# A searched start order, idle products inside the first banks, and an earlier release of v

## The chip, the cores and the metric

The kernel runs on one core of a Trainium2 chip. The metric is device time in microseconds (us), the median of several executions. One execution was also recorded by the hardware profiler; its times are counted from the start of its span.

## What is computed

Two steps follow each other. The first is a gated linear recurrence over 4 sequences of 768 tokens with 8 heads of width 48; the second is a feed-forward layer of 384 to 2048 to 384 with a GELU.

```
state = zeros(B, H, D, D)                      # B, H, S, D = 4, 8, 768, 48
for t in range(S):
    state = alpha[:, :, t, :, None] * state + einsum('bhd,bhe->bhde', k[:, :, t], v[:, :, t])
    y[:, :, t] = einsum('bhd,bhde->bhe', q[:, :, t], state)
x = y.transpose(0, 2, 1, 3).reshape(B * S, H * D)      # 3072 x 384
out = gelu_tanh(x @ w_in) @ w_out                      # w_in 384 x 2048, w_out 2048 x 384
```

## The kernel before

**Tiling.** A sequence is cut into 6 chunks of 128 tokens. A chunk of one sequence is a unit; two sequences at the same chunk are a pair, so there are 12 pairs, numbered 0 to 11, with units 0 and 1 in each. Pairs 0 and 1 are the first chunk of all four sequences.

**Steps of a pair.** Every step has a name: its kind, the pair (or block of the feed-forward layer), a dot and a running number.
- `ln` takes the logarithm of alpha (ScalarE, L359). `cum` sums it over the tokens by products (TensorE, L346 and L350 for pairs 0 and 1). `b`, `binv` and `bend` are exponentials of that sum (ScalarE, L407 and L401). `qp` and `kp` multiply q and k by them (VectorE, L418).
- `t` turns qp or kp by TensorE (L428), and `ev` copies the result out of its bank (L446, ScalarE or VectorE). In pairs 0 and 1, t 0 and 1 turn q and k of unit 0, t 2 and 3 those of unit 1, and t 4 and 5 turn k back for both units (L454, copies on L461).
- `attn` makes k times q (L489), and `mask` multiplies by a triangle (VectorE, L496; two for each unit). `vb` converts v to bf16 (L389). `y` multiplies the masked tile by vb (L546), `x` copies y out (L553), `tx` turns it (L560), `xe` copies it into the input of the feed-forward layer (L564).
- `kv` makes the state's addition (L506), `end` the factors at the chunk's end (L516), `st` the new state (L531).

**Feed-forward steps.** `l1` followed by a block number and a running number makes two of the sixteen hidden strips for one pair: six products of 256 columns (L572); `gelu` follows on ScalarE (L578). l10.0 to l10.7 is block 0 (pair 0), l11.0 to l11.7 block 1. Strips l10.0 and 1 need the first quarter of w_in, l10.2 and 3 the second, l10.4 and 5 the third, l10.6 and 7 the fourth. `l2` adds four strips into the result of one unit (L591), `ot` copies it out, `store` writes it.

**Banks.** PSUM tiles come from three rings: `ca` (1), `yk` (2 banks, shared by t, kv, y and tx) and `ff` (4 banks, shared by l1, l2, the first cums, some attn and idle products). A step that takes a bank waits until the copy that empties it is done.

**Order.** The program is recorded by a scheduler class. The order of the first 46 us or so is written out in `FIRST` (L186): each word is an engine (P TensorE, V VectorE, A ScalarE, G GpSimd, S SyncE) and a step. `fill.n` is n idle products of 512 columns of zeros into an ff bank (L289). Engines work strictly in that order, each on its own. What comes behind `FIRST` the scheduler orders by priorities and its own costs; `LANDED` (L203) tells it when loads are taken to land, for this ordering alone.

**Loads.** The twelve 192 KB loads of alpha, q and k for pairs 0 and 1 (load.0 to load.11) go out from SyncE, but for load.2 and load.3 (q and k of unit 0), which go out from ScalarE. All others go out from GpSimd in the order of `LOADS`: load.12 is v of pair 0, then come the first quarter of w_in, v of pair 1, the other quarters, w_out and the later pairs. A `gate` is a one-column copy on GpSimd (L314) out of a tile that has to have landed: what GpSimd issues behind it waits with it. `gatea 0 1` is a copy out of alpha of unit 1 of pair 0 and stands ahead of v of pair 0; `gatek 0 1` is one out of k of unit 1 and stands ahead of w_in.

Of the kernel before, what the change touches and what calls it, by code (L numbers as in the profile page):

```python
# [171 lines left out]
class _Kernel:  # L172
# [3 lines left out]

    SPLIT = (2,)
    EARLY = (0, 1)
    LOADS = ('gatea 0 1', 'v0', 'gatek 0 1', 'in 0', 'v1', 'in 1', 'in 2', 'in 3', 'out 0', 'out 1', '2a', 'out 2', '2b', 'out 3', '3', '4', '5', '6', '7', '8', '9', '10', '11')

    PACKED, CUM_FF, R = (0, 1), (0, 1), 4
    RINGS = (('a', 0, 0, 1), ('a', 0, 1, 2), ('q', 0, 0, 1), ('k', 0, 0, 1), ('q', 0, 1, 2), ('k', 0, 1, 2),
             ('a', 1, 0, 1), ('a', 1, 1, 2), ('q', 1, 0, 1), ('k', 1, 0, 1), ('q', 1, 1, 2), ('k', 1, 1, 2))
    BY_ACT = (2, 3,)

    FIRST = """  # L186
        A:table.0 A:load.2 A:load.3 S:load.0 S:load.1 S:load.4 A:ln0.0 S:load.5 P:fill.7 P:cum0.0 A:ln0.1 G:gate.0 G:load.12 S:load.6 P:cum0.1 A:b0.0 S:load.7
        A:bend0.0 V:qp0.0 A:binv0.0 A:binv0.1 S:load.8 V:kp0.0 P:fill.2 P:t0.0 A:b0.1 V:ev0.0 P:fill.1 P:t0.1 S:load.9 A:ev0.1 V:qp0.1 S:load.10 A:bend0.1
        P:fill.3 P:attn0.0 V:kp0.1 G:gate.1 S:load.11 P:t0.2 G:load.13 V:mask0.0 A:ev0.2 P:t0.3 G:load.14 V:mask0.1 A:ev0.3 P:fill.1 P:t0.4 V:ev0.4 P:fill.1
        P:attn0.1 A:ln1.0 G:load.15 P:t0.5 V:mask0.3 P:cum1.0 A:ev0.5 G:load.16 V:vb0.0 A:ln1.1 V:end0.0 P:y0.0 V:mask0.2 G:load.17 P:kv0.0 A:binv1.0 P:cum1.1  # L190
        V:st0.0 A:x0.0 G:load.18 A:vb0.1 V:kp1.0 P:tx0.0 A:b1.0 P:y0.1 V:xe0.0 G:load.19 V:qp1.0 P:t1.1 A:x0.1 A:bend1.0 G:load.20 A:b1.1 P:fill.1 P:t1.0
        A:ev1.0 V:ev1.1 G:load.21 V:qp1.1 P:fill.1 P:kv0.1 V:st0.1 G:load.22 A:binv1.1 P:tx0.1 P:attn1.0 V:xe0.1 G:load.23 P:t1.2 V:kp1.1 P:l10.0 A:ev1.2
        G:load.24 V:mask1.0 P:t1.3 A:bend1.1 P:t1.4 V:mask1.1 G:load.25 A:ev1.3 P:l10.1 V:ev1.4 G:load.26 A:vb1.0 P:t1.5 P:attn1.1 G:load.27 V:ev1.5 P:y1.0
        G:load.28 P:l10.3 V:end1.0 V:vb1.1 V:mask1.2 G:load.29 A:gelu0.0 P:kv1.0 P:l10.2 V:mask1.3 A:x1.0 G:load.30 P:l10.5 A:gelu0.1 V:st1.0 A:gelu0.3 P:y1.1
        G:load.31 P:l10.4 A:gelu0.5 V:x1.1 P:tx1.0 A:gelu0.2 P:tx1.1 P:l10.6 G:load.32 V:xe1.1 A:gelu0.4 V:xe1.0 P:l10.7 A:gelu0.6 G:load.33 P:l11.0 A:gelu0.7
        P:l11.6 A:gelu1.0 P:l11.5 A:gelu1.6 P:l11.7 A:gelu1.5 P:l11.2 A:gelu1.7 P:l11.4 A:gelu1.2 P:l11.3 A:gelu1.4 P:l11.1 A:gelu1.3 P:kv1.1 P:l20.0
        A:gelu1.1 P:l20.4 P:l20.1 A:ln2.0 P:l20.2 P:cum2.0 P:l20.5 A:b2.0 A:binv2.0 P:l20.9 A:bend2.0 V:kp2.0 A:ln2.1 P:l20.6 V:st1.1 P:cum2.1 V:qp2.0 P:l20.8
        A:b2.1 A:binv2.1 P:t2.0 P:l20.3 V:kp2.1 A:ev2.0 V:qp2.1 P:l20.10 A:bend2.1 P:attn2.0 P:t2.1 V:mask2.1 P:l20.7 A:ev2.1 V:mask2.0 P:l20.14 A:ln3.0
        P:attn2.1 P:y2.0 V:mask2.2 P:l20.13 V:mask2.3 P:l20.12 V:x2.0 P:cum3.0 A:ot0.0 V:ot0.1 P:y2.1 A:ot0.2 S:store0.0 S:store0.1 P:tx2.0 P:l20.11 A:x2.1
        S:store0.2 V:xe2.0 A:b3.0 P:tx2.1 P:l20.15 V:xe2.1 A:binv3.0 V:end2.0 P:l12.0 V:ot0.3 A:bend3.0 P:l12.1 V:qp3.0 S:store0.3 P:kv2.0 P:l12.2 V:st2.0  # L200
        A:gelu2.0 P:l12.3 V:end3.0 V:kp3.0 A:gelu2.1 P:l12.4 A:gelu2.2 P:t3.0 A:gelu2.3 P:t3.1 A:gelu2.4 V:ev3.0 P:l12.5
    """.split()
    LANDED = {"load.0": 2800, "load.1": 3400, "load.2": 4400, "load.3": 5000, "load.4": 6000, "load.5": 7300, "load.12": 10100, "load.6": 9200, "load.7":  # L203
              10000, "load.8": 10500, "load.9": 11000, "load.10": 11600, "load.11": 12000, "load.13": 14100, "load.14": 16000, "load.15":
              17800, "load.16": 19200, "load.17": 21100, "load.18": 23500, "load.19": 24800, "load.20": 26400, "load.21": 27100, "load.22":
              27900, "load.23": 28300, "load.24": 30100, "load.25": 31000, "load.26": 31900, "load.27": 32600, "load.28": 32900, "load.29":
              34800, "load.30": 36700, "load.31": 38400, "load.32": 41200, "load.33": 42600}

    NARROW = (0, 1)

# [12 lines left out]
                a=6, q=5, k=5, vb=6)  # L223
# [60 lines left out]
    def fill(self, n):  # L284
# [4 lines left out]
                self.nc.tensor.matmul(ps, self.zero[:, 0:self.C], self.zero, start=True, stop=True)  # L289
        return emit  # L290


    def load(self, n, c, i, lo=0, hi=2):

# [202 lines left out]
                                         self.ut[:, None, :].to_broadcast([self.C, self.H // 2, self.C]), op=ALU.mult)  # L497
        return emit

    def kv(self, u, i):  # L500
        nc, H, C, D = self.nc, self.H, self.C, self.D

        def emit(e):
            kv = u["kv", i] = self.tile("yk", [C, H // 2, 2 * D], F32, "kv")
            for p in range(H // 2):
                nc.tensor.matmul(kv[:, p, :], u["kn" if u["packed"] else "kp"][:, i, 2 * p:2 * p + 2, :].rearrange("t h d -> t (h d)"),  # L506
                                 u["vb"][:, i, 2 * p:2 * p + 2, :].rearrange("t h d -> t (h d)"),
                                 start=True, stop=True)
        return emit
# [25 lines left out]
    def y(self, u, i, c, b):  # L535
        nc, H, C, D = self.nc, self.H, self.C, self.D

        def emit(e):
            y = u["y", i] = self.tile("yk", [C, H, D], F32, "yps")
            if c > 0:  # L540
                st = self.state[b][c % 2]
                for p in range(H // 2):
                    nc.tensor.matmul(y[:, 2 * p:2 * p + 2, :], u["T"][:, 0, i, p, :], st[:, p, :],  # L543
                                     start=p == 0, stop=False, skip_group_check=True)
            for h in range(H):
                nc.tensor.matmul(y[:, h, :], u["atm", i][:, h % 2, h // 2, :], u["vb"][:, i, h, :],  # L546
                                 start=c == 0, stop=True, skip_group_check=True)
        return emit
# [4 lines left out]
            self.copy(e)(x, u["y", i].rearrange("t h d -> t (h d)"))  # L553
        return emit

    def turn_x(self, u, i):
        def emit(e):
            ps = u["xT_ps", i] = self.tile("yk", [self.C, self.NKT, self.C], BF16, "xT_ps")
            for j in range(self.NKT):
                self.nc.tensor.transpose(ps[:, j, :], u["x", i][:, j * self.C:(j + 1) * self.C], self.ident)  # L560
        return emit
# [57 lines left out]
    def tasks(self):  # L619
        s = self.s = Scheduler(self.BUFS, self.fill, 60000, self.FIRST, self.LANDED)  # L620
# [6 lines left out]
        loads, n, gate, held = {}, 0, [], {}  # L627
# [43 lines left out]
        for m, (c, i) in enumerate(pairs):  # L671
# [81 lines left out]
            for j in range(2):  # L753
                b, o, k, ms, turned = 2 * i + j, P + 10 + 3 * j, kp[j], masks[j], turns[j]
                at = ats[m][-1 if m not in self.SINGLE else j]
                y = s.add("y", {"PE": W["intra"] + (W["inter"] if c else 0)}, P + 20 + j, self.y(u, j, c, b),
                          ms + turned + [vin[j]] + ([states[b, c - 1]] if c else []))
                xc = s.add("x", {"ACT": W["xc_act"], "DVE": W["xc"]}, P + 20 + j, self.x(u, j), [y])
                if m in self.TURN_X:
                    xe = tx = s.add("turn", {"SP": W["turn"]}, P + 22 + j, self.turn_x_dma(u, j, c, b), [xc], xbar=W["xbar_x"], late=W["late_x"] * (m < 6))  # L760
                else:
                    tx = s.add("tx", {"PE": W["tx"]}, P + 22 + j, self.turn_x(u, j), [xc])
                    xe = s.add("xe", {"DVE": W["xe"]}, P + 22 + j, self.turned_x(u, j, c, b), [tx])
                    tx.take("yk", xe)
                y.take("yk", xc)
                xc.take("x", tx)
                users += [at, y]
                ms[0].take("atm", y)
                xts[c, b], ys[b, c] = xe, y
                vs.append(y)  # L770
                if c < NCH - 1:
                    if u["packed"]:
                        tb = s.add("t", {"PE": W["t4"]}, P + 29 + j, self.turn_back(u, j), turned)
                        k = s.add("ev", {"DVE": W["ev4"], "ACT": W["ev4_act"]}, P + 29 + j, self.turned_back(u, j), [tb])
                        tb.take("yk", k)
                        users.append(tb)
                        backs.append(tb)
                    kv = s.add("kv", {"PE": W["kv"]}, P + 30 + j, self.kv(u, j), [k, vin[j]])
                    st = states[b, c] = s.add("st", {"DVE": W["st" if c else "st0"]}, P + 30 + j, self.carry(u, j, c, b),
                                              [kv, end] + ([states[b, c - 1], ys[b, c - 1]] if c else []))  # L780
                    kv.take("yk", st)
                    vs.append(kv)
                    kvs.append(kv)
                    cs.append(st)
# [136 lines left out]
```

## Time and profile before

| | |
|---|---|
| median of 6 runs | 177.3 us (176.57 to 178.02) |
| profiled execution | 178.02 us |
| its span | 176.3 us |
| TensorE busy | 170.8 us (97%) |
| ScalarE, VectorE, GpSimd busy | 128.9, 96.4, 57.7 us |
| longest groups | l1 products (L572) 69.7 us, l2 products (L591) 69.0 us |
| DMA | 28.86 MB, mean 164 GB/s |

The span is the stretch that the profiler records; 1.7 us of the execution's time lie outside it. In the lists below, "x6" is the number of instructions put together in a row, and what stands in brackets is the idle time ahead of the row on its engine, with what ended it. In the DMA views q0 is GpSimd's queue, q1 SyncE's and q10 ScalarE's.

### The profile page before, as it was taken

The page shows a single profiled execution, that of the slowest core. Times are in us where ns is not written, and L with a number is a line of the kernel's source. Part 1 is how long each engine was busy: PE and PEld are TensorE (multiplying, and loading weights), DVE is VectorE, ACT ScalarE, POOL GpSimd, SP SyncE. Part 2 cuts the span into 40 slices and gives each one's busy share as a digit, 9 for nine tenths or more (in the row PEclk, how much of TensorE's full clock was granted, in tenths as well). Part 3 has the DMA queues.
Part 4 walks back from the last instruction along what each step waited for, and adds up shares of the span by engine and source line. Part 5 has one row for each costly group of instructions (what it writes and reads, how often), then busy time and mean ns, then how long its engine had stood idle before and what let it go on. Part 6 is the DMA issues. An engine that isn't in the chain of part 4 may idle for free.

```text
span 176.3 us, 4440 instructions
## 1 busy us (share of the span) xinstructions
PE 170.8 (97%) x1845; PEld 135.0 (77%) x1845; DVE 96.4 (55%) x192; ACT 128.9 (73%) x213; POOL 57.7 (33%) x64
## 2 busy tenths in 40 slices
PE   7899899999999999999999999999999999999993
PEld 2566799666986897797698688688697697796973
DVE  6499820166878995696499797494436405000000
ACT  4678979756968667858788967987988984481841
POOL 2495347996646766576620000000000000000000
PEclk9999999999999999999999999999999999999999
DMA  4999999999999999999999991271271360301102
GB/s 142 309 247 202 210 244 235 234 218 203 235 292 206 237 259 222 208 226 205 195 259 232 204 159 52 58 172 53 47 176 38 89 164 4 105 29 45 48 0 89
DMA packets 49620, 28.86 MB, mean 164 GB/s; under 512 B 37696, under 2 KB 46016, under 8 KB 49600
## 3 DMA queue, kind: packets, MB, share of 16 engines
q0 software_dynamic: 26464, 17.70, 60.8%
q1 hardware_dynamic: 22592, 10.49, 23.3%
q10 hardware_dynamic: 544, 0.39, 0.8%
q8 instruction: 14, 0.23, 0.5%
q14 instruction: 6, 0.05, 0.1%
HBM read 25.17 MB, written 4.72 MB: 170 GB/s over the span
## 4 chain that ended last, share of the span: by engine, by line
PE 86%; DMA 9%; POOL 2%; SPq 1%; issue 0%; ACT 0%; POOLq 0%
PE acc L591 36%; PE hT L572 35%; DMA w_in<-in_moe_w_in_dram 6%; PE at L489 3%; DMA k<-in_k_dram 3%; PE qkT_ps L428 3%; PE yps L546 2%; PE yps L543 2%; PE cum L378 2%; PE kv L506 2%; SPq L305 1%; PE xT_ps L560 1%; POOL w_in L321 1%; PE cum L380 1%; POOL v L308 1%
## 5 line engine op out<-in xcount | busy, mean ns | idle before, releaser
L572 PE MATMUL hT<-xT,w_in 128*128 128x256 bf16 x576 | 69.7, 273 | 0.5 <-DMA w_in<-in_moe_w_in_dram 0.5
L578 ACT ACTIVATE gT<-hT 128x512 bf16<-128x512 f32 x96 | 56.5, 598 | 18.5 <-PE hT L572 15.1
L591 PE MATMUL acc<-w_out,gT 128*128 128x384 bf16 (+3 forms) x416 | 69.0, 313 | 0.0
L572 PEld LDWEIGHTS <-w_in 128*128 128x128 bf16 x576 | 61.0, 114 | 2.5 <-DMA w_in<-in_moe_w_in_dram 0.9
L591 PEld LDWEIGHTS <-gT 128*128 128x128 bf16 x416 | 36.9, 97 | 19.2
L496 DVE TENSOR_TENSOR atm<-at,ut 128x512 bf16<-128x512 f32 x48 | 30.1, 681 | 12.7 <-PE at L489 12.6
L418 DVE TENSOR_TENSOR qp<-q,b 128x768 bf16<-128x768 f32 (+1 forms) x15 | 11.9, 794 | 13.9 <-ACT b L407 13.8
L418 DVE TENSOR_TENSOR kp<-k,binv 128x768 bf16<-128x768 f32 (+1 forms) x15 | 11.9, 792 | 11.1 <-ACT binv L407 10.6
L603 ACT COPY ot<-acc 128x384 f32<-128x384 f32 (+3 forms) x17 | 7.4, 439 | 13.0 <-PE acc L591 12.9
L308 POOL DMA_DIRECT2D k<-in_k_dram x11 | 12.2, 1108 | 7.5 <-DVE atm L496 2.3
L308 POOL DMA_DIRECT2D q<-in_q_dram x11 | 12.2, 1108 | 6.7 <-DVE qp L418 1.3
L308 POOL DMA_DIRECT2D a<-in_alpha_dram x11 | 12.2, 1114 | 5.5 <-DMA w_in<-in_moe_w_in_dram 1.3
L308 POOL DMA_DIRECT2D vb<-in_v_dram x11 | 12.1, 1104 | 5.1 <-DMA a<-in_alpha_dram 2.3
L407 ACT ACTIVATE b<-cum 128x768 bf16<-128x768 f32 (+1 forms) x15 | 10.3, 685 | 3.2 <-PE cum L380 2.3
L280 ACT ACT_TABLE_LOAD x9 | 11.5, 1283 | 0.9 <-PEq L905 0.7
L578 ACT ACT_TABLE_LOAD x9 | 11.5, 1283 | 0.2
L407 ACT ACTIVATE binv<-cum 128x768 bf16<-128x768 f32 (+1 forms) x15 | 10.2, 682 | 0.0
L528 DVE TENSOR_TENSOR stmp<-kv,st 128x384 f32<-128x384 f32 x16 | 8.8, 552 | 2.0 <-PE kv L506 2.0
L553 DVE CAST x<-yps 128x384 bf16<-128x384 f32 x12 | 6.7, 556 | 5.8 <-PE yps L546 5.7
L446 ACT COPY qkT<-qkT_ps 128x512 bf16<-128x512 bf16 (+1 forms) x9 | 6.5, 728 | 4.1 <-PE qkT_ps L428 4.1
L531 DVE TENSOR_TENSOR st<-stmp,ends 128x384 bf16<-128x384 f32 x16 | 8.9, 558 | 0.6
L546 PE MATMUL yps<-vb,atm 128*128 128x48 bf16 x192 | 8.7, 183 | 0.1
(65 smaller groups left out, 155.7 us busy)
## 6 DMA issues: line engine op xcount, KB each, us to landing
out_dram<-ot SPq DMA_DIRECT2D x19, 192.0 KB, 4.8
a<-in_alpha_dram POOLq DMA_DIRECT2D x9, 384.0 KB, 11.7
q<-in_q_dram POOLq DMA_DIRECT2D x9, 384.0 KB, 11.6
k<-in_k_dram POOLq DMA_DIRECT2D x9, 384.0 KB, 11.6
vb<-in_v_dram POOLq DMA_DIRECT2D x9, 192.0 KB, 11.7
w_in<-in_moe_w_in_dram POOLq DMA_DIRECT2D x4, 384.0 KB, 10.0
w_out<-in_moe_w_out_dram POOLq DMA_DIRECT2D x4, 384.0 KB, 11.4
out_dram<-ot SPq DMA_DIRECT2D x9, 96.0 KB, 1.8
```

The costliest lines, as they stand in the source:

```text
L280: nc.scalar.add_instruction(mybir.InstLoadActFuncSet(name=nc.get_next_instruction_name(), act_func_set_id=i, engine=mybir.EngineType.Activ ...
L308: dma(u[t][:, lo:hi].rearrange("t b h d -> t (b h) d"), src.rearrange("b h s d -> s (b h) d")[c * C:(c + 1) * C])
L407: self.nc.scalar.activation(u[n].rearrange("t i h d -> t i (h d)")[:, lo:hi], cum, AF.Exp, scale=1.0 if n == "b" else -1.0)
L418: self.nc.vector.tensor_tensor(out, rows, b, op=ALU.mult)
L496: self.nc.vector.tensor_tensor(u["atm", i][:, o], u["at", i][o], self.ut[:, None, :].to_broadcast([self.C, self.H // 2, self.C]), op=ALU.mult)
L528: nc.vector.tensor_tensor(s, acc, old, op=ALU.add)
L531: nc.vector.tensor_tensor(new.rearrange("f p (o d) -> f (p o) d", o=2), acc.rearrange("f p (o d) -> f (p o) d", o=2), ends, op=ALU.mult)
L546: nc.tensor.matmul(y[:, h, :], u["atm", i][:, h % 2, h // 2, :], u["vb"][:, i, h, :], start=c == 0, stop=True, skip_group_check=True)
L572: self.nc.tensor.matmul(h[:, s], w_in[:, j, nt % 4 + s], self.xT[c % self.NX][:, j, lo:hi].rearrange("p g t -> p (g t)"), start=j == 0, st ...
L578: return lambda e: self.nc.scalar.activation(self.gT[c % self.NG][:, nt:nt + 2, lo * self.C:hi * self.C], f.pop(("h", c, lo, nt)), AF.Gelu ...
L591: self.nc.tensor.matmul(f["acc", c, b][:, lo:hi], self.gT[c % self.NG][:, nt, b * self.C:(b + 1) * self.C], self.w_out[:, nt, lo:hi], star ...
L603: self.copy(e)(f["ot", c, b][:, sl], f["acc", c, b] if half is None else f["acc", c, b, half][:, sl])
```

## The change

There are four edits.
- The first gate copies out of alpha of unit 0 instead of alpha of unit 1, so v of pair 0 may be issued when the first alpha has landed.
- `FIRST` and `LANDED` are replaced. The order of the loads on SyncE, ScalarE and GpSimd stays the same up to load.48. On the other engines the start is reordered. On ScalarE ln1.0 and ln1.1 now stand ahead of ev0.2 (before: behind ev0.3 and behind ev0.5). On VectorE qp1.0 and kp1.0 stand ahead of vb0.0, mask0.2 and mask0.3. On TensorE cum1.0 and cum1.1 stand ahead of attn0.1, t1.0 ahead of y0.0, kv0.1 behind attn1.1 (before: ahead of tx0.1), and l10.0 to 7 and kv1.1 as the diff shows. Eight copies change between ScalarE and VectorE. Some steps of blocks 1 to 4 change places.
- Five single idle products (`fill.1`) are left out; fill.7, fill.2 and fill.3 stay.
- `WARM` puts idle products into the bank of the first y, kv and tx, ahead of the real ones: two ahead of each y of pair 0 and one ahead of kv0.0, of 384 columns of zeros, and four transposes of the identity ahead of each tx of pair 0. They use the bank that the step takes anyway and are overwritten by it.

The diff, cut to the rows of `FIRST` that reach into block 1:

```
-    LOADS = ('gatea 0 1', 'v0', 'gatek 0 1', 'in 0', 'v1', 'in 1', 'in 2', ...
+    LOADS = ('gatea 0 0', 'v0', 'gatek 0 1', 'in 0', 'v1', 'in 1', 'in 2', ...
...
+    WARM = {("y", 0): 2, ("kv", 0): 1, ("y", 1): 2, ("tx", 0): 4, ("tx", 1): 4}
     FIRST = """
-        A:table.0 A:load.2 A:load.3 S:load.0 S:load.1 S:load.4 A:ln0.0 S:load.5 P:fill.7 P:cum0.0 A:ln0.1 G:gate.0 G:load.12 S:load.6 P:cum0.1 A:b0.0 S:load.7
-        A:bend0.0 V:qp0.0 A:binv0.0 A:binv0.1 S:load.8 V:kp0.0 P:fill.2 P:t0.0 A:b0.1 V:ev0.0 P:fill.1 P:t0.1 S:load.9 A:ev0.1 V:qp0.1 S:load.10 A:bend0.1
-        P:fill.3 P:attn0.0 V:kp0.1 G:gate.1 S:load.11 P:t0.2 G:load.13 V:mask0.0 A:ev0.2 P:t0.3 G:load.14 V:mask0.1 A:ev0.3 P:fill.1 P:t0.4 V:ev0.4 P:fill.1
-        P:attn0.1 A:ln1.0 G:load.15 P:t0.5 V:mask0.3 P:cum1.0 A:ev0.5 G:load.16 V:vb0.0 A:ln1.1 V:end0.0 P:y0.0 V:mask0.2 G:load.17 P:kv0.0 A:binv1.0 P:cum1.1
-        V:st0.0 A:x0.0 G:load.18 A:vb0.1 V:kp1.0 P:tx0.0 A:b1.0 P:y0.1 V:xe0.0 G:load.19 V:qp1.0 P:t1.1 A:x0.1 A:bend1.0 G:load.20 A:b1.1 P:fill.1 P:t1.0
-        A:ev1.0 V:ev1.1 G:load.21 V:qp1.1 P:fill.1 P:kv0.1 V:st0.1 G:load.22 A:binv1.1 P:tx0.1 P:attn1.0 V:xe0.1 G:load.23 P:t1.2 V:kp1.1 P:l10.0 A:ev1.2
-        G:load.24 V:mask1.0 P:t1.3 A:bend1.1 P:t1.4 V:mask1.1 G:load.25 A:ev1.3 P:l10.1 V:ev1.4 G:load.26 A:vb1.0 P:t1.5 P:attn1.1 G:load.27 V:ev1.5 P:y1.0
-        G:load.28 P:l10.3 V:end1.0 V:vb1.1 V:mask1.2 G:load.29 A:gelu0.0 P:kv1.0 P:l10.2 V:mask1.3 A:x1.0 G:load.30 P:l10.5 A:gelu0.1 V:st1.0 A:gelu0.3 P:y1.1
-        G:load.31 P:l10.4 A:gelu0.5 V:x1.1 P:tx1.0 A:gelu0.2 P:tx1.1 P:l10.6 G:load.32 V:xe1.1 A:gelu0.4 V:xe1.0 P:l10.7 A:gelu0.6 G:load.33 P:l11.0 A:gelu0.7
...
+        A:table.0 S:load.0 S:load.1 A:load.2 S:load.4 A:load.3 S:load.5 S:load.6 A:ln0.0 P:fill.7 P:cum0.0 S:load.7 A:ln0.1 G:gate.0 G:load.12 S:load.8
+        P:cum0.1 A:b0.0 A:binv0.0 S:load.9 V:qp0.0 A:bend0.0 A:bend0.1 V:kp0.0 A:b0.1 P:fill.2 P:t0.0 S:load.10 A:binv0.1 V:ev0.0 P:t0.1 G:gate.1 S:load.11
+        G:load.13 A:ev0.1 V:end0.0 V:qp0.1 G:load.14 A:ln1.0 P:fill.3 P:attn0.0 V:kp0.1 P:t0.2 A:ln1.1 V:mask0.1 P:cum1.0 A:ev0.2 G:load.15 V:mask0.0 P:t0.3
+        A:b1.0 P:t0.4 P:cum1.1 V:ev0.3 G:load.16 A:binv1.0 A:ev0.4 V:qp1.0 P:t0.5 G:load.17 P:attn0.1 V:kp1.0 A:ev0.5 P:t1.0 G:load.18 V:vb0.0 A:ev1.0
+        V:mask0.2 P:y0.0 G:load.19 A:x0.0 P:t1.1 V:mask0.3 A:ev1.1 P:kv0.0 G:load.20 V:vb0.1 V:st0.0 A:binv1.1 P:y0.1 G:load.21 A:x0.1 V:kp1.1 P:tx0.0
+        G:load.22 A:bend1.0 P:tx0.1 V:xe0.0 A:b1.1 P:attn1.0 G:load.23 V:xe0.1 P:t1.3 V:qp1.1 P:l10.0 G:load.24 A:ev1.3 V:mask1.1 P:t1.2 A:bend1.1 G:load.25
+        P:t1.4 V:mask1.0 A:ev1.2 P:l10.1 G:load.26 V:ev1.4 A:vb1.0 P:t1.5 G:load.27 P:attn1.1 V:ev1.5 P:kv0.1 G:load.28 V:st0.1 G:load.29 P:l10.2 V:end1.0
+        V:mask1.3 A:gelu0.0 G:load.30 P:kv1.0 A:vb1.1 P:l10.3 V:st1.0 A:gelu0.1 P:y1.0 V:mask1.2 P:l10.4 G:load.31 A:x1.0 A:gelu0.2 P:kv1.1 P:l10.5 V:st1.1
+        A:gelu0.3 G:load.32 P:y1.1 A:gelu0.4 P:tx1.0 P:l10.6 V:x1.1 A:gelu0.5 G:load.33 V:xe1.0 P:tx1.1 P:l10.7 A:gelu0.6 V:xe1.1 P:l11.0 A:gelu0.7 P:l11.1
...
+    def warm(self, key, bank, c, b):
+        width = bank.shape[1] * bank.shape[2]
+        for _ in range(self.WARM.get((key, b), 0) if c == 0 else 0):
+            self.nc.tensor.matmul(bank, self.zero[:, 0:self.C],
+                                  self.zero[:, 0:width].rearrange("p (a b) -> p a b", a=bank.shape[1]), start=True, stop=True)
...
             kv = u["kv", i] = self.tile("yk", [C, H // 2, 2 * D], F32, "kv")
+            self.warm("kv", kv, c, b)
...
             y = u["y", i] = self.tile("yk", [C, H, D], F32, "yps")
+            self.warm("y", y, c, b)
...
             ps = u["xT_ps", i] = self.tile("yk", [self.C, self.NKT, self.C], BF16, "xT_ps")
+            for _ in range(self.WARM.get(("tx", b), 0) if c == 0 else 0):
+                self.nc.tensor.transpose(ps[:, 0, :], self.ident, self.ident)
```

## The prediction

> **What bounds the kernel now.** I read the chain of work that ended last first, because TensorE is 97% busy and the share alone does not say what it is worth.
>
> ```profile
> 2.87 5.14 DMA k<-in_k_dram
> 8.05 0.09 issue
> 8.14 0.18 POOL gate L314
> 8.32 0.29 issue
> 8.61 0.74 POOL w_in L321
> 9.35 1.17 POOL v L308
> 10.52 0.73 POOL w_in L321
> 11.25 10.56 DMA w_in<-in_moe_w_in_dram
> 21.85 0.85 PE hT L572 x6
> ```
>
> The end is set by TensorE only from 21.85 us on. Until then it is set by loads: k of unit 1 lands at 8.01, the second gate opens, GpSimd issues the quarters of w_in, and the third quarter lands 10.56 us after its issue, at 21.8. By the DMA answers for each issue the four quarters land at 15.5, 19.95, 21.8 and 23.7. The stretches show that after this nothing is free on TensorE:
>
> ```profile
> 24.00:28.00 4.00, 4.00 (x39) 4.00 (x38) 0.56 (x2) 3.38 (x7) 1.98 (x3) 1.00 1.27 239
> 60.00:100.00 40.00, 40.00 (x477) 32.72 (x476) 30.26 (x56) 31.01 (x47) 19.58 (x18) 1.00 1.38 224
> ```
>
> First number the stretch, second TensorE's busy time: equal. And TensorE's timeline shows what there is to win ahead of it:
>
> ```profile
> 16.87 0.82 PE L572 MATMUL hT<-xT,w_in 128*128 128x256 bf16 x6
> 19.98 0.84 PE L572 MATMUL hT<-xT,w_in 128*128 128x256 bf16 x6 [0.34 <-DMA w_in<-in_moe_w_in_dram]
> 21.85 0.85 PE L572 MATMUL hT<-xT,w_in 128*128 128x256 bf16 x6 [0.20 <-DMA w_in<-in_moe_w_in_dram]
> ```
>
> 0.34 and 0.20 us of waiting for weights, 0.54 in all. So the question for every edit is whether it moves a landing of w_in, or makes TensorE later than a landing.
>
> **The set of work at 21.8.** Before: l10.0, 1, 3, 2, kv0.1, kv1.0 and y1.0 are done and l10.5 starts with the third quarter. After: l10.0, 1, 2, 3, kv0.1, kv1.0 and y1.0 come ahead of l10.4, the first user of that quarter. The sets are equal. Behind it the same products follow in another order (kv1.1, 0.17 us by its row, moves from behind l11 to behind l10.4), and TensorE has no gap there. If l10.4 starts at 21.85 as l10.5 did, the end does not move.
>
> **The early v.** The gate now waits for the first alpha, which ln0.0 used at 3.82, instead of the second, at 5.2. The issue of v moves from 5.38 to about 3.95, by 1.43. The DMA view by half microseconds shows the first v packets between 8.0 and 8.5, 2.6 to 3.1 after the issue, so I expect them at 6.6 to 7.1 and the landing (6.3 after issue) at 10.25 instead of 11.7. Nobody needs it then: vb0.0 now stands on VectorE behind qp1.0 and kp1.0, which wait for q and k of pair 1. What it changes is the queue beside it:
>
> ```profile
> q1 hardware_dynamic: 228, 0.16, 99.6%
> ```
>
> This is SyncE's queue from 6.0 to 6.5 (packets, MB, share of 16 engines): it already fills the engines. Its bytes up to k of unit 1 (four loads, 0.79 MB) are through at 6.5, just before v's first bytes, so the second gate should open at 8.14 as before. The alphas of pair 1, through at 7.0 and 7.6 and landed at 8.5 and 9.1, now meet v. Bounds for the second: 9.1 if v waits; 11.4 if v takes the 0.08 to 0.11 MB per half microsecond that it took at 8.5 to 10.0 and leaves SyncE 0.03 to 0.06 of its usual 0.17 for two microseconds. The nearest row is k of pair 1, which met v before and took 6.0 us to land beside 4.8 for the load ahead of it: 1.2 more. I take 1.2 for the second alpha (10.3) and half of it for the first (9.1).
>
> The bytes ahead of w_in's third quarter are the same before and after, and the engines are full throughout; so for w_in I take no shift, with -0.3 (v's tail, which stood among the first w_in packets at 10.2 to 11.0, is gone) and +0.4 (v comes before 6.5 and delays k of unit 1) as ends. Read from the issue alone, 1.43 us earlier, it would take the whole 0.54.
>
> [...]
>
> **The new order, stage by stage.** Up to kp0.1 the starts are set by k of unit 0 (7.33) and do not move: attn0.0 at 9.07, ev0.1 to 9.0. Then ScalarE holds ln1.0 and ln1.1 ahead of ev0.2: ln1.0 from 9.1, ln1.1 from 10.3 (0.53 each by L359), ev0.2 10.8 to 11.4; before it began at
>
> ```profile
> 9.83 1.07 ACT L446 COPY qkT<-qkT_ps 128x512 bf16<-128x512 bf16 x2 [0.74 <-PE qkT_ps L428]
> ```
>
> so ev0.2 is 1.0 late, and behind it b1.0, binv1.0, ev0.4 and ev0.5. VectorE: both masks to 10.85, ev0.3 (0.68; its turn stands behind cum1.0, 0.76) to 11.6, qp1.0 after b1.0 (11.4 to 11.85) to 12.4, kp1.0 to 12.85, vb0.0 (0.35) to 13.2. So y0.0 at 13.25 instead of 12.46; two masks (1.28) and vb0.1, and the bank that ev1.1 frees, give y0.1 at about 15.1 instead of 13.99; x0.1, tx0.1 at 16.3 instead of 16.05; attn1.0, t1.3 and xe0.1, then l10.0 at 17.4 instead of 16.87. The loss shrinks because cum1, the exponentials and the turns of pair 1 are already done by then. From l10.0: 0.65 + t1.2 and t1.4 0.45 + l10.1 0.65 + t1.5 0.22 + attn1.1 0.33 + kv0.1 0.17 = 2.47, so TensorE reaches l10.2 at 19.87, and the second quarter lands at 19.95. Then 0.65 + kv1.0 0.17 + 0.65 + y1.0 0.20 end at 21.62, 0.2 ahead of the third quarter. The late start is paid out of the two waits, and nothing reaches the end.
>
> **Idle products.** Five single ones between 7.2 and 15.6 go (0.216 each by two in 0.43 at 6.57: 1.08). Added: two of 384 columns ahead of each y (0.16 each by columns), one ahead of kv0.0 (0.16), four transposes ahead of each tx (0.22 per four by L428). Those for y0.0 are covered by the wait for vb0.0; those for y0.1 mostly by mask0.3; kv0.0 and the tx ones start only when their bank opens, so 0.16 + 0.44 = 0.60 lies on the way to l10.0 and is in the 17.4. Without a cover left, the whole 1.25 would come, 0.65 more.
>
> Whether they keep the array quick: in this trace the first seven take 3.17 us, 453 ns each, later ones 216, while the granted clock reads 1.00 in both. From 9.0 to 17.0 the products after are three attn of 0.33, seven turns of 0.22, two cum of 0.76, two y of 0.20, kv 0.17, two tx of 0.17 and the 1.25 of idle ones, 6.2 us in 8 (78%); before, the rows from 13.5 to 17.0 add up to 2.3 in 3.5 (66%) with l10.0 still at full pace; so no loss, at most 2.6 us if l10.0 to l10.3 ran at half pace. [...]
>
> **Moved evictions.** Four copies go from VectorE to ScalarE (ev0.4, ev1.1, vb1.1, ot0.3) and four the other way (ev0.3, vb0.1, ev2.0, x2.1), at 0.68 against 0.59 for an ev and 0.35 against 0.53 for a vb; those ahead of l10.0 are in the starts above. In blocks 1 to 4 the changes lie beside a full TensorE; ScalarE's ten gelus take 0.65 each from 24.65, no slower than the products feed them. I cost them at nothing; if one bank were late it would be a wait of 0.1 to 0.3.
>
> **Sum.** w_in 0, lateness at l10.2 0 to 0.1, rest 0: +0.1 on the profiled execution, 178.0 to 178.1 (span 176.3 and 1.7 around it). That run is the slowest of the six; on the median of 177.3 it is 177.4.
>
> **Rivals.** *The alphas of pair 1 become the bound* (slower). Price: from a landing of a11 at 10.4, one for one, since ln1.1 holds ev0.2, that holds attn0.1 and everything to l10.2. At 11.4 it is +1.0, with k and q late too up to 1.5: 178.3 to 178.8. For it: SyncE's queue had 99.6% of the engines when v joins; against: small packets may hold their share. *Weights land earlier* (faster): v is out of the way when w_in starts. It can pay 0.54 at most by the two waits, 176.8, and only if l10.0 is at 16.9; the bytes ahead of the third quarter are the same, which speaks against it. More needs both: landings 0.9 earlier and pair 1 early. *The array slows down*: +2.0 to 2.6, about 179.5. *No effect at all*: v is used late and idle products sit in waits; the same time as my forecast.
>
> **Numbers.** A measurement of this kernel tells about 0.5%, 0.9 us, from no change. No shift at the third quarter, either way within that: 0.64 (0.12 of it early weights). Alphas bound beyond it: 0.22, slow array or an unseen late bank 0.05. Faster beyond it 0.09. Likeliest case alone 176.8 to 178.0; with the early weights and the alphas' price 176.5 to 178.9.
>
> **What would show it.** Right: l10.4 starts at 21.6 to 22.1 behind a short wait for w_in, y0.0 near 13.3, l10.0 near 17.4, no TensorE gap after 24. Wrong: k of unit 1 landing off 8.0, w_in off 21.8, a11 after 10.6 with l10.2 behind attn1.1 instead of behind DMA, idle products of 400 ns after 6 us, or a wait on TensorE behind 24 us.

## The result, and the profile after

The changed kernel takes 177.72 us (median of 33 executions, 177.16 to 179.15); the kernel before took 177.07 (70 executions, 176.37 to 178.03). The ratio is 1.0040, 95% interval 1.0030 to 1.0051: 0.65 us slower. The forecast was 177.4, "the same". The profiled execution took 178.56 us with a span of 176.8, 0.54 more than the profiled one of before.

The chain that ended last, of the kernel after (start, duration, what):

```profile
2.86 5.13 DMA k<-in_k_dram
...
10.50 9.42 DMA w_in<-in_moe_w_in_dram
19.97 0.85 PE hT L585 x6
...
39.13 1.02 ACT qkT L455
...
44.84 0.95 DVE kp L427
46.77 0.96 DVE qp L427
```

Down to 19.97 it reads like the chain of before: k of unit 1, the gate, GpSimd's issues, w_in. New are a copy on ScalarE at 39.13 and two products on VectorE at 44.84 and 46.77, in a stretch where the chain of before stayed on TensorE. TensorE's timeline at the three strips shown for before:

```profile
16.70 0.82 PE L585 MATMUL hT<-xT,w_in 128*128 128x256 bf16 x6
19.97 0.85 PE L585 MATMUL hT<-xT,w_in 128*128 128x256 bf16 x6 [0.52 <-DMA w_in<-in_moe_w_in_dram]
21.83 0.85 PE L585 MATMUL hT<-xT,w_in 128*128 128x256 bf16 x6
```

l10.0 comes 0.17 earlier than before, l10.2 waits 0.18 longer for its weights, and l10.4 starts at 21.83, where l10.5 started at 21.85. So at the third quarter the profiled executions are level, and all of the 0.54 arises behind it. The stretches show where most of it does (first number the stretch, second TensorE's busy time); first the kernel after, then the two stretches of before that were not shown:

```profile
24.00:28.00 4.00, 4.00 (x41) 3.92 (x39) 0.92 (x3) 3.29 (x6) 1.96 (x3) 1.00 1.27 243
38.00:42.00 4.00, 3.91 (x47) 2.74 (x46) 2.85 (x6) 2.61 (x4) 2.55 (x3) 1.00 1.63 190
46.00:50.00 4.00, 3.71 (x44) 3.44 (x43) 3.48 (x8) 3.51 (x6) 2.68 (x3) 1.00 1.56 277
60.00:100.00 40.00, 40.00 (x479) 32.92 (x476) 29.57 (x53) 32.19 (x49) 19.52 (x17) 1.00 1.39 224
```

```profile
38.00:42.00 4.00, 4.00 (x52) 2.62 (x52) 2.59 (x5) 1.76 (x2) 2.56 (x3) 1.00 1.60 191
46.00:50.00 4.00, 3.99 (x48) 3.78 (x47) 3.19 (x6) 3.72 (x7) 2.88 (x3) 1.00 1.34 280
```

The prediction looked at 24 to 28 and at 60 to 100, which are still full, and at nothing between. There the new order has two holes. TensorE's timeline, kernel after:

```profile
39.75 0.36 PE L557 MATMUL yps<-vb,atm 128*128 128x48 bf16 x8
40.20 0.40 PE L498 MATMUL at<-qkT 64*128 64x128 bf16 x8
...
47.78 0.40 PE L437 MATMUL qkT_ps<-ident,qp 128*128 128x128 bf16 x4 [0.29 <-DVE qp L427]
```

The eight products of y2.0 at 39.75 issue in 0.20 (y1.1's, at 23.33, are followed at 23.54), so attn2.1 could start at 39.95; it starts at 40.20, 0.25 late, when ScalarE's copy ev2.1 of 39.13 is through. Between t2.1, the turn that this copy takes out of its bank, and attn2.1 stood the strips l20.7 and l20.14 before; now it is l20.12 and the shorter y2.0. No bracket marks this wait: the row of 39.75 is drawn 0.36 long, to 40.11, which covers 0.16 of it; starts have to be subtracted. The second is t3.0 at 47.78: the fourteen products ahead of it start at 45.80 and issue in 1.53 (0.109 each), so it is 0.45 late, of which 0.29 is marked. It waits for qp3.0. The same two places in the kernel before:

```profile
38.87 1.46 PE L591 MATMUL acc<-w_out,gT 128*128 128x384 bf16 x8
40.26 0.40 PE L489 MATMUL at<-qkT 64*128 64x128 bf16 x8
...
48.25 0.39 PE L428 MATMUL qkT_ps<-ident,qp 128*128 128x128 bf16 x4
48.65 0.40 PE L428 MATMUL qkT_ps<-ident,kp 128*128 128x128 bf16 x4
```

VectorE's timeline, kernel after and then kernel before, says why:

```profile
44.84 0.95 DVE L427 TENSOR_TENSOR kp<-k,binv 128x768 bf16<-128x768 f32 x1
45.71 0.55 DVE L538 TENSOR_TENSOR stmp<-kv,st 128x384 f32<-128x384 f32 x1
46.29 0.56 DVE L541 TENSOR_TENSOR st<-stmp,ends 128x384 bf16<-128x384 f32 x1
46.77 0.95 DVE L427 TENSOR_TENSOR qp<-q,b 128x768 bf16<-128x768 f32 x1
```

```profile
45.48 0.95 DVE L418 TENSOR_TENSOR qp<-q,b 128x768 bf16<-128x768 f32 x1
46.49 0.56 DVE L528 TENSOR_TENSOR stmp<-kv,st 128x384 f32<-128x384 f32 x1
47.08 0.56 DVE L531 TENSOR_TENSOR st<-stmp,ends 128x384 bf16<-128x384 f32 x1
47.64 0.95 DVE L418 TENSOR_TENSOR kp<-k,binv 128x768 bf16<-128x768 f32 x1
```

After, kp3.0 and st2.1 stand ahead of qp3.0, and TensorE turns q first. Before, qp3.0 was done at 46.43, and kp3.0, needed by the second turn only, cost TensorE 0.18 at that place (48.65 instead of 48.47). At the first place attn2.1 of before also started 0.09 behind the eight products ahead of it (0.163 each, through at 40.17). So what is new is 0.16 at the first hole and 0.27 at the second, 0.43 of the 0.54; where the other 0.1 arises was not found.

### The profile page after: what moved, and what is told of

Same layout as the page of the kernel before. It is cut to its first block, busy times and chain, and to the rows that moved or that the text cites. A ratio compares the mean times of both kernels' runs of the same rounds, so it can differ in the third digit from the quotient of the medians.

```text
span 176.8 us, 4456 instructions
## 1 busy us (share of the span) xinstructions
PE 170.5 (96%) x1853; PEld 135.7 (77%) x1853; DVE 96.6 (55%) x191; ACT 129.2 (73%) x214; POOL 57.7 (33%) x64
## 3 DMA queue, kind: packets, MB, share of 16 engines
q0 software_dynamic: 26464, 17.70, 60.5%
## 4 chain that ended last, share of the span: by engine, by line
PE 85%; DMA 8%; DVE 1%; POOL 1%; SPq 1%; issue 1%; ACT 1%; POOLq 0%
PE acc L604 35%; PE hT L585 34%; DMA w_in<-in_moe_w_in_dram 5%; PE at L498 3%; DMA k<-in_k_dram 3%; PE qkT_ps L437 3%; PE yps L557 2%; PE cum L387 2%; PE yps L554 2%; PE kv L516 2%; SPq L314 1%; PE xT_ps L573 1%; PE cum L389 1%; POOL v L317 1%; ACT qkT L455 1%
## 5 line engine op out<-in xcount | busy, mean ns | idle before, releaser
L616 ACT COPY ot<-acc 128x384 f32<-128x384 f32 (+3 forms) x19 | 8.4, 444 | 13.1 <-PE acc L604 11.4
L564 DVE CAST x<-yps 128x384 bf16<-128x384 f32 x13 | 7.2, 557 | 5.5 <-PE yps L557 5.4
L370 ACT ACTIVATE la<-a 128x768 f16<-128x768 f32 (+1 forms) x11 | 8.5, 786 | 0.1
## 6 DMA issues: line engine op xcount, KB each, us to landing
w_out<-in_moe_w_out_dram POOLq DMA_DIRECT2D x4, 384.0 KB, 11.3
```

The costliest lines, as they stand in the source:

```text
L370: self.nc.scalar.activation(u["la"][:, lo:hi, :, 0:self.D], u["a"][:, lo:hi], AF.Ln)
```

## The experiments

The theories that the expectations speak of: the order of blocks 1 to 4 costs about 0.5 us by these two waits; the early v can hold the second alpha of pair 1 (a11), and with it the start; the start is level because w_in is the bound; idle products lie on the way, or keep the array quick. All kernels were compared with the kernel before on the same chip.

One number orders all runs: the stretch from TensorE's first strip of the third w_in quarter (l10.4 or l10.5; the same work stands ahead of it in all of them) to the end of its last product. The start is what comes ahead of it. "Quarter lands" is when that quarter landed, to 0.1 us; it and the two columns behind it are of the one profiled execution of each kernel. "At 0.99" counts the executions whose mean granted clock was 0.99; all others had 0.998 to 1.00.

| kernel | median us | ratio to before (95%) | quarter lands | strip starts | from it to the end | at 0.99 |
|---|---|---|---|---|---|---|
| before | 177.07 | | 21.8 | 21.85 | 151.73 | 0 of 99 |
| after | 177.72 | 1.0040 (1.0030 to 1.0051) | 21.8 | 21.83 | 152.27 | 0 of 33 |
| e1 gate alone | 177.34 | 1.0002 (0.9984 to 1.0020) | 20.1 | 21.00 | 152.13* | 0 of 12 |
| e2 late gate | 177.58 | 1.0025 (1.0010 to 1.0041) | 20.3 | 21.13 | 152.18 | 0 of 12 |
| e3 no products in banks | 177.85 | 1.0030 (1.0001 to 1.0059) | 20.1 | 20.86 | 152.21 | 4 of 12 |
| e4 start of after | 177.42 | 1.0017 (0.9999 to 1.0035) | 21.0 | 21.49 | 151.72 | 0 of 12 |
| e5 rest of after | 177.60 | 1.0021 (1.0006 to 1.0036) | 20.2 | 21.02 | 152.11 | 0 of 12 |
| e6 t3.0 later | 177.69 | 1.0020 (0.9996 to 1.0044) | 21.0 | 21.14 | 151.91 | 0 of 12 |
| e7 no idle products | 178.72 (one) | | 20.4 | 22.08 | 152.18 | 1 of 1 |
| e9 lean start | 177.51 | 1.0000 (0.9973 to 1.0027) | 21.6 | 22.27 | 151.73 | 4 of 12 |
| e10 late gate, old rest | 177.16 | 0.9996 (0.9980 to 1.0011) | 20.7 | 21.11 | 151.73 | 0 of 12 |
| e11 early w_in gate | 177.35 | 1.0020 (0.9989 to 1.0051) | 20.6 | 20.69 | 151.81 | 0 of 12 |
| e12 without tx turns | 176.91 | 0.9986 (0.9967 to 1.0005) | 20.8 | 20.89 | 151.82 | 0 of 12 |
| e13 products in banks alone | 177.80 | 1.0033 (1.0017 to 1.0049) | 21.5 | 21.80 | 151.66 | 0 of 12 |

(* in it a strip at 101.27 waited 0.31 for a DMA transfer (xT from x), which no other profile shows.)

**The order of the start against the order of the rest.** e4 has the start, the gate and the idle products of after, and blocks 1 to 4 as before; e5 is the reverse. The cut lies where block 1's strips end.

```
e4:  ... P:l11.4 A:gelu1.5 
-    P:l20.1 A:gelu1.4 P:l20.0 P:l20.2 A:ln2.0 ... V:kp3.0 P:kv2.1 P:kv2.0 ... V:st2.1 ... V:qp3.0 ... P:t3.1 A:gelu2.4 P:l12.5
+    A:gelu1.4 P:l20.0 P:l20.4 P:l20.1 A:ln2.0 ... V:qp3.0 S:store0.3 P:kv2.0 ... V:kp3.0 ... P:t3.1 A:gelu2.4 V:ev3.0 P:l12.5
```

> The changed kernel (gate, idle products, order) up to the end of block 1's first layer, and from there the order of before. Theory A: both waits are gone, TensorE has no gap behind 24 us, span and time are those of before within 0.2 us. Rival C (the loss is made in the start, by idle products or by loads): still 0.5 to 0.7 us slower than before.

> The order, gate and idle products of before up to the end of block 1's first layer, and from there the order of the changed kernel. Theory A: 0.5 us slower than before, with 0.25 us ahead of attn2.1 behind ScalarE's copy and 0.45 ahead of t3.0 behind qp3.0. Rival C: the time of before within 0.2 us.

In e5 both waits are there, in e4 neither, and the stretch to the end is 152.11 against 151.72. The bracket of 0.29 ahead of t3.0 stands in all five profiles with the rest of after in which t3.0 was left in its place (after, e2, e3, e5, e7), and in none with the rest of before. So the order of the rest costs 0.4 to 0.5 whatever the start; by its ratio e5 is 0.21% (0.37 us) slower than before. Whether e4 was as fast as before its ratio leaves open (0.9999 to 1.0035), but in its profile the strip started at 21.49, though the third quarter had landed at 21.0. ScalarE's timeline of e4 names the reason:

```profile
8.71 0.53 ACT L368 ACTIVATE la<-a 128x384 f16<-128x384 f32 x1
10.09 0.52 ACT L368 ACTIVATE la<-a 128x384 f16<-128x384 f32 x1 [0.86 <-DMA a<-in_alpha_dram]
10.52 0.57 ACT L455 COPY qkT<-qkT_ps 128x512 bf16<-128x512 bf16 x1
```

This is the prediction's first rival: ln1.1 waits 0.86 for a11, landed at 10.1, and holds ev0.2 behind it. e4's attn0.0 had started 0.34 earlier than that of e10 (8.87 against 9.21), and its third-quarter strip started 0.38 later, so by these two rows the hold cost some 0.7 in this execution. The same two logarithms in the profiled execution of after did not wait, and ev0.2 followed at 9.82:

```profile
8.90 0.94 ACT L368 ACTIVATE la<-a 128x384 f16<-128x384 f32 x2
9.82 0.58 ACT L455 COPY qkT<-qkT_ps 128x512 bf16<-128x512 bf16 x1
```

**The gate by itself.** e1 is the kernel before with the early gate, e2 the kernel after with the late one.

```
e1, in before:  -LOADS = ('gatea 0 1', 'v0', ...    +LOADS = ('gatea 0 0', 'v0', ...
e2, in after:   -LOADS = ('gatea 0 0', 'v0', ...    +LOADS = ('gatea 0 1', 'v0', ...
```

> The kernel before with the first gate on alpha of unit 0, nothing else. Theory A (the loss sits in the rest order of pairs 2 and 3): v is issued 1.4 us earlier, w_in's third quarter lands at 21.8 within 0.3, span and time as before within 0.3 us, no new TensorE wait behind 24 us. Rival B (the early v costs: it takes DMA time from q and k of pair 1): 0.5 to 0.7 us slower than before, with l10.0 or a load of pair 1 late.

> The changed kernel with the first gate back on alpha of unit 1, nothing else. Theory A: same time as the changed kernel within 0.3 us, so 0.5 to 0.7 us slower than before; the waits ahead of attn2.1 (0.25) and t3.0 (0.45) stay. Rival B: the loss goes, the time is that of before.

Alone, in the old order, the gate changes nothing that is measured (1.0002); there ln1.1 stands behind ev0.5, so a late a11 would have time, though in e1's profile it was not late (9.2). Against the expectation of 21.8 within 0.3, the third quarter landed at 20.1 in e1. Of the six profiled executions with the early gate, two had a11 late (10.0 in e3, 10.1 in e4) and four at 9.2 to 9.3; of the eight with the late gate none had it behind 9.3. That the early v is what made it late fits these fourteen but is not shown by them.

With e10 (told below) the four combinations of gate and rest are there, all with the new start and its products in the banks; each ratio is to the kernel before on the same chip:

| | late gate | early gate |
|---|---|---|
| rest of before | 0.9996 (e10) | 1.0017 (e4) |
| rest of after | 1.0025 (e2) | 1.0040 (after) |

The rest adds 0.29% and 0.23%, the gate 0.21% and 0.15%. In microseconds that is some 0.45 for the rest and 0.3 for the gate. The rest's share is what the traces show too (0.45 from e10's stretch to the end to e2's). The gate's share is an estimate from the ratios alone: the intervals of e2 and after overlap, as do those of e10 and e4, so by the times it may also be nothing.

**One of the two waits taken out.** e6 puts t3.0 one strip later.

```
-        A:gelu2.0 P:t3.0 A:gelu2.1 P:l12.3 V:ev3.0
+        A:gelu2.0 A:gelu2.1 P:l12.3 P:t3.0 V:ev3.0
```

> The changed kernel with t3.0 moved behind l12.3. Theory A (the wait ahead of t3.0 is paid in full at the end): the 0.45 us ahead of t3.0 goes or falls under 0.2, span and time 0.25 to 0.45 us under those of the changed kernel. Rival E (the wait moves on: t3.1, attn3.0 or kv3.0 then wait): the time of the changed kernel, with a wait of 0.3 or more on TensorE between 47 and 55 us.

The wait at t3.0 is gone (0.19 comes up at the turn behind it), the one at attn2.1 stays at 0.24, and the stretch to the end falls from 152.2 to 151.91, 0.3 of the 0.5. The times could not show this: 1.0020, with an interval from 0.9996.

**Idle products taken out.** e3 is after with `WARM = {}`; e7 leaves out fill.2 and fill.3 as well; e9 is e4 with `WARM = {}` and the late gate. In the expectations, A2 is the theory that idle products lie on the way and the array stays quick without them, D that they keep it quick.

> The changed kernel without the idle products inside the banks of y, kv and tx. Theory A2 (idle products lie on the way to l10.0 for about 0.6 us; the array stays quick without them): l10.0 about 0.4 to 0.6 us earlier than in the changed kernel; the time 0 (where w_in is awaited) to 0.5 us lower; products of the first layer at the same pace (0.65 for six). Rival D (they keep the array quick): idle products and products of 13 to 20 us take up to twice as long and the time rises by 1 us or more.

> The changed kernel without any idle product behind the first seven (fill.2 and fill.3 left out too, none inside the banks). Theory A2: same pace of products at 9 to 20 us, time within 0.5 us of the changed kernel. Rival D: turns, masks' products and first-layer products take up to twice as long from some point between 7 and 20 us on, and the time rises by 1 us or more.

> The start order of the changed kernel, but without idle products inside the banks and with the first gate on alpha of unit 1 as before; from block 1's end on the order of before. Theory A2: second alpha of pair 1 lands at 9.2, l10.0 at 16.2 to 16.5, no waits in the rest; 0.2 to 0.5 us faster than before where w_in lands by 20.5, equal to before where it lands at 21.8; on the median 0.1 to 0.4 us faster. Rival D: slower than before by 1 us or more.

In e3's profile l10.0 came only 0.11 earlier than in after (16.59), since a11 was late in it; e9's came at 16.44, as expected. But here the second half of A2 fell, and e9 was not faster than before (1.0000). The stretches of e9 (the last number but two is the granted clock), and TensorE's timeline of it:

```profile
12.81:16.22 3.41, 2.45 (x40) 1.68 (x41) 3.27 (x9) 2.87 (x7) 2.70 (x5) 1.00 1.11 212
```

```profile
16.50:19.25 2.75, 2.75 (x20) 2.20 (x18) 1.83 (x4) 1.52 (x4) 0.97 (x2) 0.50 1.21 198
```

```profile
16.11 0.54 PE L437 MATMUL qkT_ps<-ident,kp 128*128 128x128 bf16 x4
16.44 1.49 PE L585 MATMUL hT<-xT,w_in 128*128 128x256 bf16 x6
17.72 0.63 PE L437 MATMUL qkT_ps<-ident,qp 128*128 128x128 bf16 x4
...
18.57 1.35 PE L585 MATMUL hT<-xT,w_in 128*128 128x256 bf16 x6
```

l10.0 starts at 16.44 and takes 1.49 where 0.82 is usual. By tenths of a microsecond the granted clock is half from 16.22 to 19.64, 3.41 us, after 3.41 us in which TensorE was 72% busy by the profile (2.45) and never idle for over 0.35 at a time. In e7 it is half for the same 3.41 us, from 9.39 to 12.80. It does not come in every execution: 8 of 24 in e3 and e9 have a mean clock of 0.99. In e9 these four took 177.93 to 178.45 and the other eight had a median of 177.16; in e3 178.43 to 178.77 against 177.45. Of the 117 executions of kernels that have products in the banks none had it, nor had one of the 99 of the kernel before, with its five single products, that ran beside these experiments.

A busy share alone does not decide it. Two profiled executions in which the clock did not drop (mean 1.00) have a stretch of the same length that is no busier, the first of e3, the second of e12 (told below):

```profile
12.40:15.81 3.41, 2.45 (x41) 1.80 (x41) 3.14 (x8) 3.12 (x8) 3.34 (x5) 1.00 1.13 230
```

```profile
4.45:7.87 3.42, 2.35 (x28) 1.66 (x26) 1.07 (x2) 1.96 (x7) 1.40 (x2) 1.00 1.00 312
```

Whether the place of the stretch or the kind of products in it makes the difference was not tested.

**What the products in the banks cost, and which are needed.** e13 is the kernel before, with them in place of its five single ones; e10 is e4 with the late gate; e12 is e10 without the transposes of the identity; e11 is e10 with the second gate on k of unit 0.

```
e13, in before:  -P:fill.1 (five times)   +WARM = {("y", 0): 2, ("kv", 0): 1, ("y", 1): 2, ("tx", 0): 4, ("tx", 1): 4}
e12, in e10:     -WARM = {..., ("y", 1): 2, ("tx", 0): 4, ("tx", 1): 4}   +WARM = {..., ("y", 1): 2}
e11, in e10:     -'gatek 0 1'   +'gatek 0 0'
```

> The kernel before, whole order and gates as before, but with the idle products in the banks of y, kv and tx of pair 0 in place of the five single ones. Theory: they lie partly on the way (0.6 us by the prediction's sum), so l10.0 starts 0.2 to 0.6 later than 16.9; where the third quarter of w_in lands at 21.8 nothing reaches the end, where it lands at 20 to 21 up to 0.4 us does: ratio 1.000 to 1.002. Rival (what they keep quick is worth something here): the scatter of the times shrinks and the median is 0.2 us or more below the kernel before.

> The changed kernel's order of the start with its idle products in the banks, but with v released by the second alpha as before, and the order of blocks 1 to 4 as before. Theory A (the order of blocks 1 to 4 costs 0.5 us by two waits of TensorE): both waits, 0.25 at attn2.1 and 0.45 at t3.0, are gone. Theory B (the early v can hold the second alpha of pair 1): that alpha lands at 9.2 to 9.4, and l10.0 starts at 16.7 to 16.9. Together: as fast as the kernel before, 0 to -0.3 us, ratio 0.998 to 1.000. If the start itself costs something (a rival), +0.3 to +0.5 stays.

> As the first kernel of this call, without the four transposes of the identity ahead of each tx of pair 0; the idle products ahead of y and kv stay. If the transposes count for the array's pace, some executions drop to half pace near l10.0 (six products in 1.3 to 1.5 us instead of 0.82, mean granted clock below 1.00) and the median is 0.3 to 0.8 us above the first kernel's, with more scatter. If they do not count, l10.0 takes 0.82, and starts 0.3 to 0.4 earlier than with them: 0 to -0.3.

> As the run before it, and in addition the second gate copies out of k of unit 0 (landed at 7.3) instead of k of unit 1 (8.0), so that the issue of w_in starts about 0.7 us earlier. If the landing of w_in's third quarter bounds the end, as the prediction said, the quarters land up to 0.7 earlier and the time falls by up to 0.5 us in executions in which that quarter lands at 21.8, and not at all where it lands at 20 to 21. If w_in then meets SyncE's queue (rival), k of unit 1 and the alphas of pair 1 land 0.3 to 1.0 later and l10.0 starts after 17.2: +0.3 to +1.0.

l10.0 in TensorE's timelines of e13, e10 and e12, for the last two with y0.1, the step ahead of the transposes:

```profile
17.70 0.82 PE L585 MATMUL hT<-xT,w_in 128*128 128x256 bf16 x6
```

```profile
14.87 0.36 PE L557 MATMUL yps<-vb,atm 128*128 128x48 bf16 x8
...
16.84 0.82 PE L585 MATMUL hT<-xT,w_in 128*128 128x256 bf16 x6
```

```profile
14.71 0.36 PE L557 MATMUL yps<-vb,atm 128*128 128x48 bf16 x8
...
16.47 0.82 PE L585 MATMUL hT<-xT,w_in 128*128 128x256 bf16 x6
```

In the old order the products, in place of the five single ones, cost 0.80 at l10.0 (16.90 in e1 to 17.70) and 0.6 in the median, both more than the 0.2 to 0.6 and 0 to 0.4 expected. The new order of the start takes 0.86 off again (17.70 to 16.84). Without the transposes l10.0 is 0.37 earlier, but 0.16 of that is there at y0.1 already; 0.21 is theirs. Without them none of twelve executions lost the pace, so it can be kept without them. e12 has the lowest median, 176.91 against 177.72 of after. It is not told apart from the kernel before (0.9967 to 1.0005). e11 issued the first w_in quarter at 7.3 instead of 8.75, and its first three quarters landed at 15.0, 18.8 and 20.6 against 14.6, 18.8 and 20.7 in e10: between these two executions, an issue 1.45 earlier moved none of the landings forward by more than 0.1. The times of e11 reached 179.25; why is open, since its profile is that of an execution of 176.94.

## Why the prediction was right, and where not

The time lay in the range and within 0.5%, as forecast, but not because the sum was close: the loss was 0.65 where 0.1 was summed, and the interval of the ratio (1.0030 to 1.0051) leaves the 0.1 out. One term was wrong, a second in part of the executions, and both together stayed under the 0.9 us that the forecast allowed. By the prediction's own signs, a wait on TensorE behind 24 us speaks against its mechanism, and there was one.

- **The set of work at the third quarter: right, for the executions like the profiled one.** 21.83 after, 21.85 before. But the landing of that quarter varies from 20.1 to 21.8 between profiled executions, and that both profiles fell at its late end was luck. In eight of the twelve experiments TensorE came to that strip 0.4 us or more after its weights: there its own chain is the bound: 21.00 in the old order (e1), 21.13 in the new (e2), 21.49 with a11 late (e4). "Lateness is paid out of the two waits" held only where there were waits.
- **The early v: w_in's shift 0, and k of unit 1 at 8.0, were right between the two profiles.** v landed at 10.80, not 10.25. SyncE's queue at 6.0 to 6.5 had fewer packets than the 228 of before, and v's first ones came between 7.0 and 7.5, behind all that k of unit 1 needed:

```profile
q1 hardware_dynamic: 205, 0.15, 92.0%
```

- **The alphas: a11 at 10.3 was right for e4 (10.1), wrong for the profiled execution (9.2).** Hence ev0.2 at 9.82 instead of 10.8, y0.0 at 12.98 (13.25), y0.1 at 14.72 (15.1), tx0.1 at 15.87 (16.3), l10.0 at 16.70 (17.4). The rival "the alphas become the bound" is real in part of the executions: 0.38 us at the strip (21.49 in e4 against 21.11 in e10), not the 1.0 of its upper end. In the mean it is at most the gate's 0.3 above, which the times do not tell from nothing.
- **The idle products: 0.60 on the way was of the right size** (0.80 by e13 against e1 in the old order; in the new one t1.3, ahead of l10.0, started at 16.61 in e10 and at 16.11 in e9, 0.5). "So no loss" of pace was right for the changed kernel, 0 of 33. The reason given was weak: "66% with l10.0 still at full pace" is one execution. Its 66% counts issue times, and the profile has 93% (3.26 of 3.50) for that stretch of before; the 72% of e9 is the profile's too, and comes to 46% by issue times (1.56 of 3.41).
- **The term that failed: the rest of the order, "cost at nothing".** Measured 0.4 to 0.5, nearly all by two waits, larger together than the "one bank late, 0.1 to 0.3" allowed, and given 0.05 of the chance together with the slow array. It is the larger part of the loss. The swap of kp3.0 and qp3.0, and that less work stands between t2.1 and attn2.1, were visible in the order itself; none of the eight moved copies is what TensorE waits for in the two holes. VectorE's rows would have told that qp3.0, behind kp3.0 (0.95) and st2.1 (1.1), ends at least 2 us after its inputs, on the engine that TensorE waits for next.

How often a11 is late, what makes it late, and why the landings of w_in fall early in one execution and late in another, stays open.

## What to carry to other kernels

Where an order is replaced, go through every stretch that it covers and subtract start from start on the engine that is full, not only where the stretch looks interesting: two waits of 0.25 and 0.45 us, one without a bracket, made the larger part of this result. Before trusting a landing as the bound, see whether it is the same in several executions; here it moved by 1.7 us. Idle products were insurance here (with neither those in the banks nor the five single ones 8 of 24 executions lost the pace, with those in the banks 0 of 117): judge them by the share of executions that lose the pace, not by one trace, and keep only those that this share needs.

## What the runs showed of the hardware

The array dropped to half pace (granted clock 0.50, and six products in 1.49 instead of 0.82 in e9) for 3.41 us after a stretch of equal length in which TensorE was 72% busy (e9) or 53% busy (e7: 1.81 in 3.41), with no idle time over 0.7. Stretches of 69% and 72% in e12 and e3 passed without a drop, so the share alone is no threshold. Between 10.5 and 17, the profiles of after, e10, e12 and e13 were at least 82% busy in every such stretch (2.81 in 3.41 the lowest), and none of their executions lost the pace. The same loads of w_in (the third quarter) landed from 20.1 (e1, e3) to 21.8 (before), with issue times of 11.2 to 11.3.
